# Moving the start addresses of SBUF tiles by four small pads: one operand of the matmuls at 0 modulo 128 bytes, the rest at 64

## The chip, the cores and the metric

The kernel runs on one core of a Trainium2 chip. The time is the device time of one execution in microseconds (us); lower is better. The kernel before took 1770.54 us (median of three runs, 1768.67 to 1771.02).

## The reference

Three stages follow one another; everything is float32.

```python
# 1: attention over keys and values that are means of 8 neighbours (B, H, S, D = 8, 8, 576, 64)
k_p = k.reshape(B, H, Sp, 8, D).mean(axis=3);  v_p = v.reshape(B, H, Sp, 8, D).mean(axis=3)
attn = softmax(q @ k_p.T / sqrt(D));  x = attn @ v_p          # x: 4608 tokens x 512
# 2: x (4608 x 512) -> 2048 -> 512, rational activation
h = x @ w_in
g = (a0 + a1*h + a2*h**2 + a3*h**3) / (1 + |b0|*|h| + |b1|*h**2 + 1e-6)
x = g @ w_out
# 3: 512 -> 1536 -> 512, gated
out = (silu(x @ w_gate) * (x @ w_val)) @ w_out2
```

## The kernel before

Tokens lie along the free axis in nine tiles of 512 (`TT`). A matmul has a **moving** operand, which is streamed column by column (tokens), and a **stationary** one, 128 x 128 weights, which a separate weight load brings in. In the profile's rows of a matmul the names after the arrow are the moving tile and then the stationary one: `bank<-X,W` streams X against W.

Every large product is done three times in a one-pass float32 type (`float32r`): a value is held as a high and a low part in one tile `[128, 2, 512]`, and high x high, high x low and low x high are added up in a PSUM bank. Each of these matmuls reads one contiguous row of 512 columns (2,048 bytes) in each partition of the moving tile, or 256 columns (1,024 bytes) where a stage works on half a token tile. The small matmuls of the attention use plain float32.

There are three phases:

- **Phase 1**, the attention and the second stage of the reference. For each of nine token tiles and 16 slices of the hidden axis (144 steps), 12 matmuls of `proj_ops` stream X against a W tile (`bank<-X,W`, line 473), a chain of ACT, POOL and DVE operations (`moe1_ops`, lines 525 to 547) makes the activation in a tile G, and two steps later 12 matmuls of `acc_ops` stream G against a W tile (`bank<-G,W`, line 473). The attention units (`unit_ops`, `unit_out_ops`; lines 402, 439, 455) for the next token tile, and the conversion of weights (`bits_ops`, `seven_ops`), are put between them.
- **Phase 2** (`pair_ops`, line 684): gate and value projections on pairs of token tiles, in a seven-product scheme. The moving tiles are split tokens; they lie in a ring of slots, X4 to X7 and then fourteen of the W tiles. The stationary tiles lie in the other W tiles, in X0 to X3, in G and in one tile We. So all pairings occur: W against X, W against W, X against X, X against W and a few with G and We.
- **Phase 3** (`out_ops`, line 785): the last projection, with the same slots.

The order of all instructions is set beforehand by a planner (`Plan`): each operation has a due time and a list of engines with costs, and the planner writes one fixed order for each engine. It knows nothing of addresses. All DMAs are issued from SP's queue in that order.

Tiles get their addresses from the order in which they are allocated. `low` (from the bottom) holds `ident`, three small tiles, `X0` to `X7` and the W tiles of the first weight matrix; `low_al` holds the attention's tiles and later W tiles; `const` holds `SA`, `SB`, `SC`, `RAW`, `ST`, four kinds of small tiles, `G0`, `G1` and the W tiles of the second matrix; `al` the last W tiles. Nearly every tile is a multiple of 128 bytes long in a partition, so what a few small tiles leave over is handed on from tile to tile:

```python
    qc = low.tile([128, 1], F32, name="qc")
    X = [low.tile([128, 2, TT], F32R, name=f"X{i}") for i in range(8)]
...
    SM = [const.tile([128, 8, 2], F32, name=f"SM{i}")[:, :, 0:1] for i in range(2)]
    G = [const.tile([128, 2, TT], F32R, name=f"G{i}") for i in range(NG)]
```

The statement that issues nearly all of TensorE's time in phase 1, with w the weights and x the moving tile:

```python
        for j, (i0, i1) in enumerate(((0, 0), (0, 1), (1, 0))):
            nc.tensor.matmul(out=out, lhsT=w[:, i0, wc], rhs=x[:, i1, :],
                             start=first and j == 0, stop=last and j == 2)
```

The diff touches only the allocations at the top of `tile_pooled_attention_moe_moe2`; that function is long, and of it only the pieces above and in the diff matter here.

Of the kernel before, what the change touches and what calls it, by code (L numbers as in the profile page):

```python
# [8 lines left out]
F32 = mybir.dt.float32  # L9
# [61 lines left out]
class Plan:  # L71
# [22 lines left out]
    def op(self, due, alts, r=(), w=()):  # L94
        i = len(self.ops)
        deps = set()
        for k in r:
            if k in self.writer:
                deps.add(self.writer[k])
        for k in w:  # L100
            if k in self.writer:
                deps.add(self.writer[k])
            deps.update(self.readers.get(k, ()))
        deps.discard(i)
        self.ops.append((due, alts, deps))
        for k in w:
            self.writer[k] = i
            self.readers[k] = []
        for k in r:
            self.readers.setdefault(k, []).append(i)  # L110
# [59 lines left out]
def dve(n, fn, port=False, fast=1, ptrs=0):  # L170
    return ("DVE", n / (0.96 * fast) + 66 + 60 * ptrs, 0, port, fn)


def pool(n, fn):
    return ("POOL", 2.1 * n + 145, 0, True, fn)
# [6 lines left out]
def pe(ns, fn):  # L182
    return ("PE", ns, 0, False, fn)
# [3 lines left out]
def tile_pooled_attention_moe_moe2(  # L187
# [18 lines left out]
    low = ctx.enter_context(tc.tile_pool(name="low", bufs=1))  # L206
    low_al = ctx.enter_context(tc.tile_pool(name="low_al", bufs=1))
    const = ctx.enter_context(tc.tile_pool(name="const", bufs=1))
# [8 lines left out]
    ab = low.tile([128, 6], F32, name="ab")  # L217
    babs = low.tile([128, 2], F32, name="babs")
    qc = low.tile([128, 1], F32, name="qc")
    X = [low.tile([128, 2, TT], F32R, name=f"X{i}") for i in range(8)]  # L220
    SCR = tuple(range(32 - NSCR, 32))
    first_use = {f: n for n, (t, f, _, _) in reversed(list(enumerate(SEQ)))}
    need1 = sorted([(first_use[f], "in", f) for f in range(NF1)] + [(first_use[f] + 2, "out", f) for f in range(NF1)])
# [2 lines left out]
    def W(i):  # L226
        if W_[i] is None:
            p = (low_al if i in SCR else low) if need1[i][1] == "in" else (al_p if i in SCR else const)
            W_[i] = p.tile([128, 2, 512], F32R, tag=f"W{i}", name=f"W{i}")
        return W_[i]  # L230
# [5 lines left out]

    scr_tile, scr_keys = {}, {i: [] for i in SCR}

    def scratch(i, key):
        if i not in scr_tile:  # L240
            p = low_al if need1[i][1] == "in" else al_p
            scr_tile[i] = p.tile([128, 1024], F32, tag=f"W{i}", name=f"scr{i}")
        scr_keys[i].append(key)
        return scr_tile[i]
# [7 lines left out]
    MX = [const.tile([128, 8, 1], F32, name=f"MX{i}") for i in range(2)]  # L252

    SM = [const.tile([128, 8, 2], F32, name=f"SM{i}")[:, :, 0:1] for i in range(2)]
    G = [const.tile([128, 2, TT], F32R, name=f"G{i}") for i in range(NG)]
    for i in range(32 - NSCR):
        W(i)
    kpbd = low_al.tile([128, 8, 2, SP], F32, tag="kpbd", name="kpbd")
# [5 lines left out]
    QBS, SSS, ATS = [(QB, "q0")], [(SS, "s0")], [(AT, "at0")]  # L264
    i = SCR[-1]
    QBS.append((scratch(i, "q1")[:, 0:TT], "q1"))
# [15 lines left out]
    class Ring:  # L282
# [17 lines left out]
    first_raw = Ring([  # L300
        (scratch(i, f"fraw{i}").bitcast(I32).rearrange("p (a t) -> p a t", t=2), f"fraw{i}") for i in SCR[4:-3]
    ])
    first_st = Ring(st_all[0:4] + [
        (scratch(i, f"fst{i}{j}")[:, 512 * j:512 * j + 512], f"fst{i}{j}") for i in SCR[0:4] for j in range(2)
    ])
# [54 lines left out]
    def kv_ops(due, bb, hp):  # L360
# [8 lines left out]
        def folds(x, out):  # L369
            for n in (4, 2):  # L370
                P.tensor_tensor(out=x[:, :, 0:n], in0=x[:, :, 0:n], in1=x[:, :, n:2 * n], op=ALU.add)
            P.tensor_tensor(out=out, in0=x[:, :, 0], in1=x[:, :, 1], op=ALU.add)

        op(due, [dve(S, lambda: V.tensor_reduce(out=kt, in_=kr, axis=AX.X, op=ALU.add)),
                 ("POOL", 2.1 * 7 * SP + 435, 0, True, lambda: folds(kr, kt))],
           [], [kk, f"kt{hp % 2}"])
        for h in range(2):
# [5 lines left out]

        op(due + V_POOL, [dve(1024, lambda: V.tensor_reduce(out=vps[:, c], in_=vr, axis=AX.X, op=ALU.add)),
                          ("POOL", 2.1 * 7 * 128 + 435, 0, True, lambda: folds(vr, vps[:, c]))],
           [], [kv, f"vp{c}"])

    def unit_ops(due, t, hp, pa, u=0):
# [4 lines left out]
        m = hp % 2  # L393
        mx, sm = MX[m], SM[m]
        (qb, kq), (ss, ks), (at_, ka) = QBS[u], SSS[u], ATS[u]
        kps = [f"kp{kv_slot(bb, hp)}{h}" for _, _, bb in segs(t, 0, TT) for h in range(2)]
        op(due - Q_DMA, [dma(1 << 18, lambda: sync.dma_start(out=qb, in_=qT[hp, :, t * TT:(t + 1) * TT]))], w=[kq])
        for i in range(2):
# [13 lines left out]
            def peak(g=g, src=src):  # L412
                V.tensor_reduce(out=mx[:, g, :], in_=src, axis=AX.X, op=ALU.max, negate=True)  # L413

# [31 lines left out]
    def unit_out_ops(due, t, hp, pa, u=0):  # L446
# [12 lines left out]

        x = X[(t % 2) * 4 + hp]  # L460
        xk = f"X{(t % 2) * 4 + hp}"
        op(d, [pe(930, pv)], [ka + "a", ka + "b"] + vks, [k0])
# [8 lines left out]
    def mm3(out, w, wc, x, first, last):  # L471
# [4 lines that stand above are left out]
    def proj_ops(due, bk, e, x0):  # L476
        wkey, get = w_tile[e]
        for kt in range(4):
            op(due, [pe(648, lambda kt=kt: mm3(
                bank[bk], get(), slice(kt * 128, kt * 128 + 128), X[x0 + kt], kt == 0, kt == 3))],  # L480
               [wkey + "h", wkey + "l", f"X{x0 + kt}h", f"X{x0 + kt}l"], [f"bank{bk}"])

    def acc_ops(due, e, g, first, last):
        wkey, get = w_tile[e]
        for dt in range(4):
            op(due, [pe(648, lambda dt=dt: mm3(
                bank[PY[dt]], get(), slice(dt * 128, dt * 128 + 128), G[g], first, last))],
               [wkey + "h", wkey + "l", f"G{g}h", f"G{g}l"], [f"bank{PY[dt]}"])

# [26 lines left out]
    def moe1_ops(n):  # L516
        t, f, _, _ = SEQ[n]
        i, g, bk = n % NSC, n % NG, (4 + n % 2 if n < N_SW else 4 + n % 3)
        A, Bt, C, gt, hb = SA[i], SB[i], SC[i], G[g], bank[bk]
        kA, kB, kC, kh = f"A{i}", f"B{i}", f"C{i}", f"bank{bk}"  # L520
        proj_ops(n, bk, ("in", f), (t % 2) * 4)
        if n >= 2:
# [14 lines left out]
            out=gt[:, 0, :], in0=hb, scalar=ab[:, 0:1], in1=Bt, op0=ALU.add, op1=ALU.mult), ptrs=1)],  # L537
           [kh, kB], [f"G{g}h"])
        op(d, [dve(512, lambda: V.scalar_tensor_tensor(  # L539
            out=C, in0=C, scalar=QC, in1=gt[:, 0, :].bitcast(F32), op0=ALU.add, op1=ALU.mult), True)],  # L540
           [f"G{g}h"], [kC])
        op(d, [dve(512, lambda: V.scalar_tensor_tensor(  # L542
# [3 lines left out]
        def low(eng):  # L546
            return lambda: eng.tensor_tensor(out=gt[:, 1, :], in0=A, in1=Bt, op=ALU.mult)  # L547

        op(d, [pool(512, low(P)), dve(512, low(V), True)], [kA, kB], [f"G{g}l"])

# [281 lines left out]
    def w1_ops(i, due, e):  # L832
        if i in SCR:
            op(due, [("NONE", 0, 0, False, lambda: None)], [], scr_keys[i] + [f"W{i}h", f"W{i}l"])
        early = i < 32 - NSCR
        w_ops(due, e, lambda: W(i), f"W{i}", first_raw if early else mid_raw, first_st if early else mid_st)
# [191 lines left out]
```

## Time and profile before

| | |
|---|---|
| median of three runs | 1770.54 us (1768.67 to 1771.02) |
| the profiled execution | 1771.74 us, span 1770.0 us |
| TensorE (PE) busy | 1711.5 us, 97% of the span, 8,100 matmuls |
| weight loads (PEld) busy | 1388.5 us, beside the matmuls |
| VectorE (DVE), ScalarE (ACT), GpSimd (POOL) busy | 1355.1, 1081.5, 512.8 us |
| mean granted TensorE clock | 0.991 of full speed |
| DMA | 283.17 MB, 48.5% of 16 engines over the span |

The busy time of an engine is the union of its instructions, and matmuls overlap in their pipeline: the row of one matmul lasts some 389 ns, while the next one starts earlier. How fast the matmuls follow each other is read from a row of the timeline that merges a run of them, as (length of the run - length of one) / (count - 1).

### The profile page before, as it was taken

The numbers are of one execution on the slowest core, as the hardware profiler recorded it, in microseconds if no ns is written. First come the engines' busy times: TensorE is split into PE (matmuls) and PEld (weight loads), VectorE is DVE, ScalarE is ACT, GpSimd is POOL, SyncE is SP. The second block draws the span as 40 slices with busy tenths as digits, with TensorE's granted clock in tenths as the row PEclk, the third lists the DMA queues.
The fourth block names the chain that finished last, engine by engine and source line by source line (L and its number), as shares of the span: only waits on it lengthen the run. The fifth ranks groups of instructions, "written<-read, shape, count | busy, mean of one in ns | idle before, by whom it ended". The sixth has DMA issues, their size and how long they took to land.

```text
span 1770.0 us, 24470 instructions
## 1 busy us (share of the span) xinstructions
PE 1711.5 (97%) x8100; PEld 1388.5 (78%) x8100; DVE 1355.1 (77%) x2201; ACT 1081.5 (61%) x2324; POOL 512.8 (29%) x424
## 2 busy tenths in 40 slices
PE   5899899999999999999999999999999999999999
PEld 3567677777777787777788777888889888888888
DVE  7899998989989898988999667346354536778874
ACT  7777777777777786777677554334343424545543
POOL 4556463534545362333435121000000000101100
PEclk9799999999999999999999999999999999999999
DMA  8412343514334251313136889546456887755642
GB/s 278 151 42 72 112 145 108 172 45 144 112 116 139 93 158 36 102 49 107 60 119 213 279 281 322 165 143 202 157 173 221 285 265 250 272 182 193 217 135 84
DMA packets 139711, 283.17 MB, mean 160 GB/s; under 512 B 14656, under 2 KB 44864, under 8 KB 139584
## 3 DMA queue, kind: packets, MB, share of 16 engines
q1 hardware_dynamic: 139584, 281.60, 48.5%
q8 instruction: 64, 1.05, 0.2%
q14 instruction: 63, 0.52, 0.1%
HBM read 197.14 MB, written 84.41 MB: 159 GB/s over the span
## 4 chain that ended last, share of the span: by engine, by line
PE 76%; DVE 11%; DMA 6%; ACT 4%; issue 2%; POOL 0%; SPq 0%; DVEq 0%; ACTq 0%; POOLq 0%
PE bank L473 33%; PE bank L684 23%; PE bank L785 15%; DMA wodr<-RAW 2%; PE bank L402 2%; PE bank L455 2%; DVE SC L539 2%; PE bank L439 1%; DVE G L536 1%; DVE SA L542 1%; DVE SA L531 1%; DMA RAW<-in_k 1%; DVE G L547 1%; DVE bank L532 1%; DMA X<-wdr 1%
## 5 line engine op out<-in xcount | busy, mean ns | idle before, releaser
L473 PE MATMUL bank<-X,W 128*128 128x512 f32 x1728 | 442.8, 401 | 7.5 <-DVE SA L542 7.5
L473 PE MATMUL bank<-G,W 128*128 128x512 f32 x1728 | 429.6, 394 | 0.6 <-POOL W L335 0.6
L473 PEld LDWEIGHTS bank<-X,W 128*128 128x128 f32 x1728 | 322.5, 191 | 88.3 <-DVE SA L542 11.5
L473 PEld LDWEIGHTS bank<-G,W 128*128 128x128 f32 x1728 | 319.7, 188 | 72.1 <-issue 5.6
L528 POOL TENSOR_TENSOR SC<-SC,SB 128x512 f32<-128x512 f32 x144 | 198.6, 1379 | 319.0 <-ACT SC L526 317.5
L684 PE MATMUL bank<-W,X 128*128 128x512 f32 (+1 forms) x972 | 213.6, 366 | 3.7 <-ACT SA L693 1.4
L684 PEld LDWEIGHTS bank<-W,X 128*128 128x128 f32 x972 | 169.3, 189 | 35.6 <-ACT ST L693 2.2
L684 PE MATMUL bank<-W,W 128*128 128x512 f32 (+1 forms) x816 | 181.0, 367 | 4.0 <-ACT SB L693 3.0
L785 PE MATMUL bank<-W,W 128*128 128x512 f32 (+1 forms) x840 | 174.8, 365 | 0.0
L684 PEld LDWEIGHTS bank<-W,W 128*128 128x128 f32 x816 | 142.1, 189 | 30.7 <-ACT SB L693 4.0
L785 PEld LDWEIGHTS bank<-W,W 128*128 128x128 f32 x840 | 145.2, 189 | 25.3
L534 ACT ACTIVATE SB<-SC,qc 128x512 f32<-128x512 f32 x144 | 104.6, 726 | 66.8 <-POOL SC L528 66.3
L536 DVE SCALAR_TENSOR_TENSOR G<-bank,ab,SB 128x512 fp32r<-128x512 f32 x144 | 107.4, 746 | 38.8 <-PE bank L473 22.1
L525 ACT ACTIVATE SB<-bank 128x512 f32<-128x512 f32 x144 | 86.0, 597 | 70.5 <-DVE G L547 46.0
L539 DVE SCALAR_TENSOR_TENSOR SC<-SC,G 128x512 f32<-128x512 f32 x144 | 120.6, 837 | 3.8
L526 ACT ACTIVATE SC<-SB,babs 128x512 f32<-128x512 f32 x144 | 117.8, 818 | 0.1
L529 ACT ACTIVATE SA<-bank,ab 128x512 f32<-128x512 f32 x144 | 112.3, 780 | 0.1
L331 POOL TENSOR_TENSOR ST<-ST,ST 128x512 int32<-128x512 int32 x53 | 75.2, 1419 | 115.5 <-DVE ST L328 94.2
L532 DVE SCALAR_TENSOR_TENSOR bank<-SA,ab,bank 128x512 f32<-128x512 f32 x144 | 107.6, 748 | 1.2
L542 DVE SCALAR_TENSOR_TENSOR SA<-bank,ab,SC 128x512 f32<-128x512 f32 x144 | 106.9, 743 | 0.7
L531 DVE TENSOR_TENSOR SA<-SA,bank 128x512 f32<-128x512 f32 x144 | 97.7, 679 | 7.7 <-ACT SA L529 7.4
L417 ACT ACTIVATE QS<-bank,MX 128x72 f32<-128x72 f32 x272 | 83.7, 325 | 21.6 <-DVE MX L413 21.2
(227 smaller groups left out, 2611.5 us busy)
## 6 DMA issues: line engine op xcount, KB each, us to landing
X<-wdr SPq DMA_DIRECT2D x105, 512.0 KB
wdr<-ST SPq DMA_DIRECT2D x84, 256.0 KB
RAW<-sdr SPq DMA_DIRECT2D x56, 256.0 KB
X<-sdr SPq DMA_DIRECT2D x48, 256.0 KB
wodr<-RAW SPq DMA_DIRECT2D x42, 256.0 KB
RAW<-in_w_out SPq DMA_DIRECT2D x19, 512.0 KB
RAW<-in_k SPq DMA_DIRECT2D x32, 288.0 KB
RAW<-in_v SPq DMA_DIRECT2D x32, 288.0 KB
```

The lines of the kernel that those rows point to most:

```text
L473: nc.tensor.matmul(out=out, lhsT=w[:, i0, wc], rhs=x[:, i1, :], start=first and j == 0, stop=last and j == 2)
L526: op(d, [act(512, False, lambda: A_.activation(out=C, in_=Bt, func=AF.Identity, scale=babs[:, 1:2], bias=babs[:, 0:1]), 2)], [kB, "ab"], [kC])
L528: op(d, [pool(512, lambda: P.tensor_tensor(out=C, in0=C, in1=Bt, op=ALU.mult))], [kB], [kC])
L529: op(d, [act(512, True, lambda: A_.activation(out=A, in_=hb, func=AF.Identity, scale=ab[:, 3:4], bias=ab[:, 2:3]), 2)], [kh, "ab"], [kA])
L531: op(d, [dve(512, lambda: V.tensor_tensor(out=A, in0=A, in1=hb, op=ALU.mult))], [kh], [kA])
L532: op(d, [dve(512, lambda: V.scalar_tensor_tensor(out=hb, in0=A, scalar=ab[:, 1:2], in1=hb, op0=ALU.add, op1=ALU.mult), ptrs=1)], [kA], [kh])
L534: op(d, [act(512, False, lambda: A_.activation(out=Bt, in_=C, func=AF.Ln, bias=qc), 1)], [kC], [kB])
L536: op(d, [dve(512, lambda: V.scalar_tensor_tensor(out=gt[:, 0, :], in0=hb, scalar=ab[:, 0:1], in1=Bt, op0=ALU.add, op1=ALU.mult), ptrs=1)], ...
L539: op(d, [dve(512, lambda: V.scalar_tensor_tensor(out=C, in0=C, scalar=QC, in1=gt[:, 0, :].bitcast(F32), op0=ALU.add, op1=ALU.mult), True)] ...
L542: op(d, [dve(512, lambda: V.scalar_tensor_tensor(out=A, in0=hb, scalar=ab[:, 0:1], in1=C, op0=ALU.add, op1=ALU.subtract), ptrs=1)], [kC, k ...
L684: nc.tensor.matmul(out=bk, lhsT=gw()[:, i0, m:m + 128], rhs=gx()[:, i1, 0:n], start=first and kk == 0 and q == 0, stop=kk == 1 and q == 2, ...
L785: nc.tensor.matmul(out=bk, lhsT=gw()[:, g % 2, c:c + 128], rhs=gx()[:, i1, 0:n], start=first and g == 0 and q == 0, stop=g == NFP - 1 and ...
```

## The change

Four pads are allocated and never used: 32 bytes ahead of X, 64 bytes behind X, 64 bytes ahead of G and 64 bytes behind G.

```diff
@@ -217,7 +217,10 @@
     qc = low.tile([128, 1], F32, name="qc")
+
+    low.tile([128, 8], F32, name="pad0")
     X = [low.tile([128, 2, TT], F32R, name=f"X{i}") for i in range(8)]
+    low.tile([128, 16], F32, name="pad1")
     SCR = tuple(range(32 - NSCR, 32))
@@ -252,7 +255,9 @@
     SM = [const.tile([128, 8, 2], F32, name=f"SM{i}")[:, :, 0:1] for i in range(2)]
+    const.tile([128, 16], F32, name="pad2")
     G = [const.tile([128, 2, TT], F32R, name=f"G{i}") for i in range(NG)]
+    const.tile([128, 16], F32, name="pad3")
     for i in range(32 - NSCR):
```

The start addresses in a partition, modulo 128 bytes, in the two built programs:

| tile | before | after |
|---|---|---|
| X0 to X7 | 96 (X0 at 1760) | 0 (X0 at 1792) |
| G0, G1 | 96 | 0 |
| all W tiles, We | 96 | 64 |
| kpbd, vps, QS, AT (attention), scratch | 96 | 64 |
| SA, SB, SC, RAW, ST | 96 | 64 |
| KT0, KT1 | 96, 0 | 64, 96 |
| MX0, MX1; SM0, SM1 | 32, 64; 96, 32 | 0, 32; 64, 0 |
| ident | 0 | 0 |

No instruction is added, removed or moved: the rows of every engine's order, DMAs on SP's queue included, are the same in both programs but for buffer and line numbers. So no excerpt of an order stands here.

## Rows read from the trace of the kernel before

**Rows 1.** The page's part 1: busy time, share of the span, instructions of each engine.

```profile
PE 1711.5 (97%) x8100; PEld 1388.5 (78%) x8100; DVE 1355.1 (77%) x2201; ACT 1081.5 (61%) x2324; POOL 512.8 (29%) x424
```

**Rows 2.** Busy time by stretch: phase 1, phase 2, phase 3.

```profile
core 0: us, PE busy (x) PEld busy (x) DVE busy (x) ACT busy (x) POOL busy (x), PEclk, DMA share, GB/s
33.00:987.00 954.00, 920.94 (x4274) 725.47 (x4273) 864.85 (x1369) 717.37 (x1601) 446.49 (x368) 0.98 0.36 114
987.00:1508.00 521.00, 513.09 (x2484) 431.06 (x2482) 271.52 (x464) 210.88 (x397) 35.88 (x30) 1.00 0.68 227
1508.00:1770.00 262.00, 258.64 (x1260) 219.19 (x1258) 195.87 (x325) 129.38 (x231) 18.50 (x12) 1.00 0.55 179
```

**Rows 3.** The chain that ended last, pieces: start us, us, what.

```profile
860.73 76.52 PE bank L473 x336
...
1507.93 258.72 PE bank L785 x1260
```

**Rows 4.** PE's timeline, runs of 19 (512 columns) and 49 (256 columns).

```profile
1711.77 4.47 PE L785 MATMUL bank<-W,W 128*128 128x512 f32 x19
...
1749.20 6.04 PE L785 MATMUL bank<-W,W 128*128 128x256 f32 x49
```

**Rows 5.** Groups of PE's matmuls by form, lines 473, 684 and 785: busy us, mean ns.

```profile
L473 PE MATMUL bank<-X,W 128*128 128x512 f32 x1728 | 442.8, 401 | 7.5 <-DVE SA L542 7.5
L473 PE MATMUL bank<-G,W 128*128 128x512 f32 x1728 | 429.6, 394 | 0.6 <-POOL W L335 0.6
L684 PE MATMUL bank<-W,X 128*128 128x512 f32 x756 | 183.5, 390 | 2.6 <-ACT SA L693 1.4 <-ACT ST L693 0.6 <-ACT SC L693 0.6
...
L785 PE MATMUL bank<-W,W 128*128 128x512 f32 x648 | 150.8, 389 | 0.0
L684 PE MATMUL bank<-X,X 128*128 128x512 f32 x252 | 67.5, 389 | 0.1
L684 PE MATMUL bank<-X,W 128*128 128x512 f32 x228 | 61.3, 390 | 0.0
L785 PE MATMUL bank<-X,W 128*128 128x512 f32 x216 | 51.9, 389 | 0.0
L402 PE MATMUL bank<-kpbd,QS 128*128 128x144 f32 x240 | 44.8, 305 | 7.6 <-ACT kpbd L379 5.3 <-ACT QS L417 1.8 <-DVE X L466 0.3
L439 PE MATMUL bank<-ident,QS 128*72 128x128 f32 x272 | 42.1, 284 | 23.2 <-POOL QS L431 16.1 <-DVE QS L431 4.6 <-ACT SB L525 1.9
...
L785 PE MATMUL bank<-W,W 128*128 128x256 f32 x192 | 24.0, 283 | 0.0
```

**Rows 6.** PE's timeline, with idle time before; then 54.9 to 57.7 us: timeline, group, stretch.

```profile
47.62 1.92 PE L439 MATMUL bank<-ident,QS 128*72 128x128 f32 x8 [8.07 <-POOL QS L431]
...
54.27 4.04 PE L473 MATMUL bank<-X,W 128*128 128x512 f32 x9
...
L473 PE MATMUL bank<-X,W 128*128 128x512 f32 x9 | 4.0, 628 | 0.0
...
54.90:57.70 2.80, 2.80 (x9) 2.13 (x8) 2.80 (x6) 1.90 (x10) 0.62 (x2) 0.50 0.10 41
```

**Rows 7.** PE's timeline, plain float32: transposes (line 439), scores (line 402).

```profile
503.64 0.60 PE L439 MATMUL bank<-ident,QS 128*72 128x128 f32 x4
...
519.47 0.65 PE L402 MATMUL bank<-kpbd,QS 128*128 128x144 f32 x4
```

**Rows 8.** Groups by line: a DVE operation of phase 1, idle before it, releasers.

```profile
L536 DVE SCALAR_TENSOR_TENSOR G<-bank,ab,SB 128x512 fp32r<-128x512 f32 x144 | 107.4, 746 | 38.8 <-PE bank L473 22.1 <-ACT SB L535 5.7 <-ACT SB L525 4.1
```

**Rows 9.** PE's timeline in phase 2: pairings side by side.

```profile
1450.56 0.84 PE L684 MATMUL bank<-X,X 128*128 128x512 f32 x3
1451.24 0.84 PE L684 MATMUL bank<-W,X 128*128 128x512 f32 x3
```

**Rows 10.** PE's timeline, groups of 12 in phase 1.

```profile
511.13 3.06 PE L473 MATMUL bank<-X,W 128*128 128x512 f32 x12
...
516.75 2.88 PE L473 MATMUL bank<-X,W 128*128 128x512 f32 x12
```

## The prediction

> **What bounds the kernel now.** I read the engines' shares first: PE is busy 97% of the span, the next engine, DVE, 77% [rows 1]. By stretch, PE is the bound in all three phases, but in phase 1 DVE stands close behind it: of 954.0 us PE is busy 920.94 and DVE 864.85; in phase 3 PE is busy throughout and DVE has room [rows 2]. The chain of waits agrees: phase 3 is one piece of 258.72 us of matmuls, and in phase 1 there are pure stretches too, 336 matmuls in 76.52 us [rows 3]. So what the change does to a matmul counts, and the question is how fast matmuls follow each other.
>
> That is read from merged runs. 512 columns: (4.47 - 0.389) / 18 = 0.2267 us. 256 columns: (6.04 - 0.283) / 48 = 0.1199 us [rows 4, 5]. The difference is 106.8 ns for 256 columns, 0.417 ns a column, which is 2.4 GHz. What is left over is 226.7 - 213.3 = 13.3 ns for the long form and 119.9 - 106.7 = 13.3 ns for the short one: **a fixed 13.3 ns per matmul, whatever its length**. There are 6,480 long and 756 short ones in the three phases (lines 473, 684, 785; the largest groups are in [rows 5]), so it costs 7,236 x 13.3 = 96 us in all.
>
> Two rows tell what kind of cost it is. From 54.3 us the granted clock is 0.50, the 1.2 GHz level (PE had stood idle for 8.07 us shortly before), and the same matmul follows after (4.04 - 0.628) / 8 = 426.5 ns [rows 6]: 512 columns at 1.2 GHz are 426.7 ns, so there the extra is gone. And the plain float32 forms take (0.60 - 0.284) / 3 = 105 ns for 128 columns and (0.65 - 0.305) / 3 = 115 ns for 144 [rows 5, 7], about 0.8 ns a column or half the column rate, with no 13 ns on top though each loads its weights too. So the extra is not the hand-over from one matmul to the next. It appears only where 4-byte columns are streamed at full rate, and points at the reading of the operands from SBUF.
>
> **My theory.** At 2.4 GHz 13.3 ns are 32 columns, or 128 bytes of float32. A row of 2,048 bytes that starts at 96 modulo 128 touches 17 blocks of 128 bytes, not 16; one of 1,024 bytes touches 9, not 8: 17 x 32 columns are 226.7 ns and 9 x 32 are 120.0 ns, which are both rows. If the moving row is fetched in such blocks and nothing can run ahead at full rate, a start at 0 gives the extra back, and a start at 64 does not. No row shows it, since all moving tiles of these matmuls start at 96 now.
>
> **The change part by part.** It adds no instruction and moves none; the pads cost nothing in time.
>
> *X and G to 0.* The gain of one matmul lies between 0 (the extra has another cause) and 13.3 ns (all of it goes). The nearest rows are the transposes and scores, where at most 2 or 3 ns can hide in the rounding of the rows [rows 7]; I take 13.3 less about 2, so 11 ns.
>
> Phase 1: 1,728 + 1,728 matmuls [rows 5] x 11 = 38.0 us. Not all will land. DVE's idle time there is 954.0 - 864.85 = 89 us and would shrink to 51, 94% busy, in a fixed order. For it speaks that part of DVE's idle time is itself a wait for PE (22.1 us ahead of line 536 [rows 8]). What is late next is G for the second 12 matmuls. Between 0 and 38 I take two thirds, 25 us.
>
> Phases 2 and 3: moving tiles in X slots are 252 + 228 and 216 long matmuls [rows 5], and seven smaller groups (with G or We, or of 256 columns) add 168: 864 x 11 = 9.5 us. Those of phase 3, 288 x 11 = 3.2 us, land whole, as the chain there is PE alone [rows 3]; of the rest, 6.3 us, I take 5, since the start of phase 2 has gaps that no matmul fills (521.0 us against 513.09 busy [rows 2]). Together 8 us. Moving tiles in W slots (756 and 648 are the largest groups) stay at 226.7 ns.
>
> *Stationary tiles from 96 to 64.* A weight load of 512 bytes touches 5 blocks of 128 either way. I cost it at nothing; what covers it is the matmul beside it (PEld is busy 725.47 us of 954.0 [rows 2]). Bounds: the rivals below, from 5,124 x 11 ns less to 26 us more.
>
> *The tiles of DVE, ACT, POOL and the DMAs from 96 to 64.* Every pairing of tiles on those engines but X and G keeps equal offsets. I cost it at nothing within 2 us either way; the cover is PE, and where DVE's 6% are used up it would show in phase 1.
>
> Sum: 1771.74 - 25 - 8 = 1738.7 us for the profiled execution; this stood 1.2 us above the median of the runs, so **1737.5 us**. The likeliest case's own range: 1771.7 - 47.5 = 1724 where all lands, down to 1753 with 10 us in phase 1 and 7 behind it, or **1722 to 1755**.
>
> **The rivals.**
>
> *Nothing changes (1770.5 us).* The extra belongs to the one-pass float32 form at full clock, wherever its rows start. For it: it is the same for every pairing, in every slot and under every load of the other engines (three matmuls take 0.84 us, or one every 226 ns, for X against X and for W against X [rows 9]). Against it: nothing with another start is among them, so the rows can't tell. The change would then do what it says and be worth nothing. The Trainium skill, "SBUF — State Buffer", section "Specifications (TRN2)", speaks for this rival: the line of SBUF is 16 bytes there, 96, 64 and 0 all start a line, and by that the time would stay at 1770.5. The other way speaks "TensorE: Matmul & The Clock Gate" of the Trainium skill, section "Wait — 56ns, not 53.3ns?": warm matmuls of 512 columns follow after 215.7 ns, and cold ones after exactly N / 1.2 GHz. The cold row agrees (426.5), the warm one does not (226.7). By that page the gain is an estimated 11.0 ns.
>
> *Opposite halves decide (1729 us).* The moving and the stationary row disturb each other where both start at the same offset, and the extra goes wherever they now differ by 64: 3,456 in phase 1, and in phases 2 and 3 W against X 756, X against W 228 + 216, G or We against the other kind 168, short forms 300. That is 1,668 x 11 = 18.3 us behind phase 1, of which 16 land: 1770.5 - 25 - 16. For it: the change keeps its two kinds of tile 64 apart. Against it: the extra has no spread, as two streams that collide at chance should give.
>
> *Any multiple of 64 is enough (1707 us).* All 7,236 matmuls gain: 25 us in phase 1 and 3,780 x 11 = 41.6, of which 38 land.
>
> *Slower (1796 us).* With the two streams at different offsets the weight load takes turns from the stream that it didn't take before, in phase 1 above all, where all 288 groups of 12 have this pairing. The price is bounded below by 0 and above by the slow groups that are there already: 3.06 against 2.88 us for 12 matmuls [rows 10], 0.18 us more, x 288 = 52 us. I take half, 26 us. It decides from 0.012 us per group on, which is 3.5 us or 0.2% of the time.
>
> **How the numbers follow.** Chances: the forecast 0.28, opposite halves 0.15, any multiple of 64 0.14, nothing 0.25, slower 0.18. Of the 0.25 for nothing, 0.01 drifts faster and 0.03 slower by over 0.2%, about what a measurement of this kernel can tell from no change. So faster 0.28 + 0.15 + 0.14 + 0.01 = 0.58, same 0.21, slower 0.18 + 0.03 = 0.21. The range, 1700 to 1782 us, takes in the three gains with their bounds but for the lowest end of the 64 rule, no change, and the mild part of the slower case; about 0.2 is left out.
>
> **What would show it.** Right, if in the profile after: the groups of 12 in phase 1 (X against W, G against W) follow every 215 to 216 ns, a group 2.76 instead of 2.88 us; X against X and X against W do so in phases 2 and 3; and W against X and W against W stay at 226.7. If W against X falls and X against X does not, opposite halves decide; if all fall, 64 is enough. Phase 1 should shrink by some 25 us with DVE at 93% of it. I am wrong if the run of 49 short matmuls and all others still follow every 120.0 and 226.7 ns, or if groups in phase 1 take over 2.9 us.

## The result, and the profile after

The changed kernel takes 1792.58 us (median of four runs, 1788.68 to 1796.16) against 1769.61 us for the kernel before, beside it. The ratio is 1.0123, with a 95% interval of [1.0106, 1.0139]: it is **slower by 23 us**, where 33 us less was forecast. The profiled execution took 1796.16 us, with a span of 1794.4.

The page's part 1 after, then busy time by stretch (phases 1, 2, 3, cut where they end in this trace):

```profile
PE 1739.6 (97%) x8100; PEld 1390.6 (77%) x8100; DVE 1358.6 (76%) x2201; ACT 1081.7 (60%) x2324; POOL 515.6 (29%) x424
```

```profile
35.00:999.00 964.00, 933.32 (x4278) 726.01 (x4277) 869.14 (x1369) 717.54 (x1603) 448.55 (x368) 0.99 0.35 113
999.00:1527.50 528.50, 520.86 (x2481) 430.41 (x2480) 270.43 (x464) 210.90 (x397) 36.53 (x30) 1.00 0.67 224
1527.50:1794.00 266.50, 263.57 (x1261) 219.54 (x1259) 196.24 (x325) 129.25 (x232) 18.55 (x12) 1.00 0.53 175
```

Against [rows 1] only PE has become busier, by 28 us; DVE, ACT, POOL and the weight loads differ by 3.5 us or less. Against [rows 2] phase 1 is longer by 10.0 us, phase 2 by 7.5 and phase 3 by 4.5; the start is later by 2 us. The granted clock is the same to 0.01. So all three phases pay, and they pay on PE.

The chain that ended last after, two pieces that answer to [rows 3]:

```profile
869.27 78.43 PE bank L478 x336
...
1527.65 263.44 PE bank L790 x1260
```

The same 336 matmuls took 76.52 us before, the same 1,260 took 258.72. Nothing waits in these stretches: the matmuls themselves follow each other more slowly. PE's timeline after (start us, us, engine, line, operation, count), in phases 1, 2 and 3:

```profile
883.33 2.95 PE L478 MATMUL bank<-G,W 128*128 128x512 f32 x12
886.12 2.96 PE L478 MATMUL bank<-X,W 128*128 128x512 f32 x12
...
1091.36 5.62 PE L689 MATMUL bank<-X,X 128*128 128x512 f32 x24
...
1471.75 0.86 PE L689 MATMUL bank<-X,X 128*128 128x512 f32 x3
...
1739.82 5.96 PE L790 MATMUL bank<-W,W 128*128 128x512 f32 x25
...
1749.82 2.96 PE L790 MATMUL bank<-W,G 128*128 128x512 f32 x12
...
1760.98 9.42 PE L790 MATMUL bank<-W,W 128*128 128x256 f32 x78
```

A group of 12 in phase 1 takes 2.95 to 2.96 us, where the quick groups before took 2.88 [rows 10]: per matmul (2.96 - 0.398) / 11 = 233 ns against (2.88 - 0.39) / 11 = 226 ns. W against W takes (5.96 - 0.394) / 24 = 231.9 ns, W against G 233 ns. Only the short form is a little quicker, (9.42 - 0.282) / 77 = 118.7 ns against 119.9 [rows 4]. (The last one's length in these sums, 0.389 to 0.398 us for long and 0.276 to 0.283 for short, here and below, is the mean of its form in the trace.)

The surprise is that **hardly any pairing is spared**: moving tiles at 0 are as slow as those at 64, and so are W against W, both at 64. Long runs of X against X do keep the quick pace, 24 in 5.62 us or one every (5.62 - 0.393) / 23 = 227.3 ns; in threes between other pairings they are slow as well, 0.86 us where three took 0.84 [rows 9]. That kills the theory of the prediction at once, but says neither whether the moving start, the stationary start or their relation decides, nor why W against W is slow too.

### The profile page after: what moved, and what is told of

Its sections match the earlier page's. It is cut to its first block, busy times and chain, and to the rows that moved or that the text cites. A ratio compares the mean times of both kernels' runs of the same rounds, so it can differ in the third digit from the quotient of the medians.

```text
span 1794.4 us, 24470 instructions
## 1 busy us (share of the span) xinstructions
PE 1739.6 (97%) x8100; PEld 1390.6 (77%) x8100; DVE 1358.6 (76%) x2201; ACT 1081.7 (60%) x2324; POOL 515.6 (29%) x424
## 4 chain that ended last, share of the span: by engine, by line
PE 79%; DVE 11%; DMA 6%; ACT 3%; issue 2%; POOL 0%; SPq 0%; DVEq 0%; ACTq 0%; POOLq 0%
PE bank L478 36%; PE bank L689 23%; PE bank L790 15%; DMA wodr<-RAW 2%; PE bank L460 2%; PE bank L407 2%; PE bank L444 1%; DVE SC L544 1%; DVE G L541 1%; DVE SA L547 1%; DMA RAW<-in_k 1%; DVE SA L536 1%; DMA ydr<-ST 1%; DMA sdr<-ST 1%; DMA X<-wdr 0%
## 5 line engine op out<-in xcount | busy, mean ns | idle before, releaser
L478 PE MATMUL bank<-X,W 128*128 128x512 f32 x1728 | 448.0, 404 | 7.2 <-DVE SA L547 7.2
L478 PE MATMUL bank<-G,W 128*128 128x512 f32 x1728 | 437.1, 398 | 0.6 <-POOL W L340 0.6
L689 PE MATMUL bank<-W,W 128*128 128x512 f32 (+1 forms) x816 | 183.9, 370 | 3.9 <-ACT SB L698 2.2
L790 PE MATMUL bank<-W,W 128*128 128x512 f32 (+1 forms) x840 | 178.0, 368 | 0.0
L531 ACT ACTIVATE SC<-SB,babs 128x512 f32<-128x512 f32 x144 | 117.8, 818 | 0.1
```

What stands on the lines that cost most here:

```text
L531: op(d, [act(512, False, lambda: A_.activation(out=C, in_=Bt, func=AF.Identity, scale=babs[:, 1:2], bias=babs[:, 0:1]), 2)], [kB, "ab"], [kC])
L689: nc.tensor.matmul(out=bk, lhsT=gw()[:, i0, m:m + 128], rhs=gx()[:, i1, 0:n], start=first and kk == 0 and q == 0, stop=kk == 1 and q == 2, ...
L790: nc.tensor.matmul(out=bk, lhsT=gw()[:, g % 2, c:c + 128], rhs=gx()[:, i1, 0:n], start=first and g == 0 and q == 0, stop=g == NFP - 1 and ...
```

## The experiments

Every kernel here is the kernel before with other pads (or a few edited lines), and with the same order of instructions. `px` and `pw` stand for the bytes of the pads ahead of and behind X, `pg` and `pq` for those ahead of and behind G; the change is 32, 64, 64, 64.

```diff
+    low.tile([128, px // 4], F32, name="pad0")
     X = [low.tile([128, 2, TT], F32R, name=f"X{i}") for i in range(8)]
+    low.tile([128, pw // 4], F32, name="pad1")
...
+    const.tile([128, pg // 4], F32, name="pad2")
     G = [const.tile([128, 2, TT], F32R, name=f"G{i}") for i in range(NG)]
+    const.tile([128, pq // 4], F32, name="pad3")
```

### Which start counts: the moving one, the stationary one, or both

**X and G at 96, the rest at 64** (0, 96, 32, 96).

> X and G stay at 96 modulo 128, all W, attention and scratch tiles go to 64: in phase 1 only the stationary row's start is changed. Moving theory (a long matmul is slow, about 232 instead of 227 ns, when its moving row starts at a multiple of 64): phase 1 (moving X, G) as before at 228 ns; in phases 2 and 3 the W-moving groups at 232, the X-moving ones at 227; about 1781 us. Stationary theory (the same of the stationary row): phase 1 at 232 to 233, W against X at 227, W against W and X against W at 232; about 1793 us. Relation theory (slow when the two starts differ modulo 128): phase 1 and all mixed pairings slow, W against W and X against X at 227; about 1792 us.

1797.13 us, ratio 1.0148 [1.0128, 1.0167]. PE's timeline in phases 1 and 3, and a piece of its chain:

```profile
876.45 2.97 PE L476 MATMUL bank<-G,W 128*128 128x512 f32 x12
879.26 2.97 PE L476 MATMUL bank<-X,W 128*128 128x512 f32 x12
...
1714.77 16.27 PE L788 MATMUL bank<-W,W 128*128 128x512 f32 x69
```

```profile
1528.73 264.34 PE bank L788 x1260
```

**X and G at 0, the rest at 96** (32, 96, 32, 96).

> X and G go to 0 modulo 128, everything else stays at 96. Moving theory: phase 1 at 232 to 233 ns, X-moving groups slow, W-moving ones at 227; about 1789 us. Stationary theory: phase 1 as before at 228, W against X and X against X at 232, W against W at 227; about 1775 us. Relation theory: phase 1 and mixed pairings slow, W against W and X against X at 227; about 1792 us.

1795.07 us, ratio 1.0138 [1.0118, 1.0158]. Timeline and chain:

```profile
877.48 2.97 PE L477 MATMUL bank<-G,W 128*128 128x512 f32 x12
880.28 2.97 PE L477 MATMUL bank<-X,W 128*128 128x512 f32 x12
```

```profile
1524.39 264.34 PE bank L789 x1260
```

These two have no start in common that the other theories could use: modulo 128, once only the stationary tile left 96, once only the moving one. Yet they behave alike, 2.97 us a group and 264.34 us for phase 3 in both. What they share is the difference: moving minus stationary is 32 modulo 128 in both. The moving theory and the stationary theory each missed one of the two by 15 us or more; the relation theory had phase 1 right, but W against W, both at 64, is slow here as well: (16.27 - 0.39) / 68 = 233.5 ns.

**Everything at 0** (32, 0, 0, 0).

> Every large tile at 0 modulo 128, so all pairings have equal starts. Moving theory and stationary theory: all long matmuls at 231 to 233 ns, about 1793 us as with the change. Relation theory: all at 227, about 1770 us. The theory of the prediction (blocks of 128 bytes) would have had 215 ns, and 1707 us.

1769.52 us, ratio 0.9997 [0.9982, 1.0013]: the kernel before again, with X and G exactly where the change puts them. Timeline and chain:

```profile
873.34 2.88 PE L474 MATMUL bank<-G,W 128*128 128x512 f32 x12
876.06 2.88 PE L474 MATMUL bank<-X,W 128*128 128x512 f32 x12
```

```profile
1509.29 258.72 PE bank L786 x1260
```

**Everything at 32** (64, 0, 0, 0).

> Every large tile at 32 modulo 128. If an odd multiple of 32 is what makes the fast state, by the moving or the stationary start: all long matmuls at 227, about 1770 us. Relation theory: the same 1770 us. If the distance to the next multiple of 128 counts (96 is the only good start): slow, 1785 us or more.

1772.56 us, ratio 1.0012 [0.9997, 1.0026]. The chain:

```profile
861.28 76.52 PE bank L474 x336
...
1507.82 258.72 PE bank L786 x1260
```

Both pieces are those of [rows 3] to the hundredth. So where the tiles lie is of no account; **that all of them start alike is what counts**. At 0 the long form follows after the same 226.7 ns as at 96, so a start at a multiple of 128 gives nothing back.

### Alike modulo what

W against W in the change was slow with both at 64 modulo 128. Modulo 256 they are not alike: the four pads leave the W tiles of the lower pools at 64 and those of the upper pools at 192 (X is at 0, G at 128). The pads of the two slow runs above split them too, into 64 and 192 and into 96 and 224. Three kernels test this.

**X and G 128 bytes after all W** (0, 128, 128, 128).

> Moving tiles X and G start 128 bytes further than all W tiles (X 224, G 224, W 96 modulo 256). If the two starts need only be equal modulo 128: every long matmul at 227 ns, about 1770 us. If they must be equal modulo 256: phase 1 at 232 to 234 ns, mixed pairings in phases 2 and 3 slow, W against W at 227 away from the mixed ones; about 1790 us.

1787.27 us, ratio 1.0101 [1.0081, 1.0120]. Timeline in phases 1 and 3, and chain:

```profile
877.05 2.96 PE L476 MATMUL bank<-G,W 128*128 128x512 f32 x12
...
1720.49 2.96 PE L788 MATMUL bank<-X,W 128*128 128x512 f32 x12
...
1727.44 7.88 PE L788 MATMUL bank<-W,W 128*128 128x512 f32 x34
```

```profile
1521.73 260.92 PE bank L788 x1260
```

A difference of 128 is slow, and W against W, now alike modulo 256, is back at (7.88 - 0.39) / 33 = 227.0 ns.

**The change, with all W at 64 modulo 256** (32, 64, 192, 64).

> The change with one difference: modulo 256 X and G start at 0 and all W tiles at 64, where the change has X 0, G 128, the W tiles of the lower pools 64 and those of the upper pools 192. Modulo 128 both kernels are the same. If equality modulo 128 counts: no difference to the change, 1792 us, and W against W stays at 232. If modulo 256: phase 1 stays at 232 to 233 (moving and stationary differ by 64 in both), but W against W, 1,284 long matmuls in phases 2 and 3, falls to 227 where it follows its own kind; up to 6.4 us less, about 1786 to 1789 us.

1789.88 us, ratio 1.0116 [1.0087, 1.0145]. Timeline in phase 3, and chain:

```profile
1651.36 1.54 PE L789 MATMUL bank<-W,W 128*128 128x512 f32 x6
...
1655.54 17.86 PE L789 MATMUL bank<-W,W 128*128 128x512 f32 x78
1673.24 2.96 PE L789 MATMUL bank<-X,W 128*128 128x512 f32 x12
```

```profile
1524.01 260.54 PE bank L789 x1260
```

W against W: (17.86 - 0.39) / 77 = 226.9 ns; X against W beside it stays at 2.96 us. Six of W against W between two groups of X against W are not quick yet, (1.54 - 0.39) / 5 = 230 ns: the disturbance outlasts the pairs that cause it, and a like pair is quick only some matmuls later. Phase 3 is 2.9 us shorter than with the change. The whole time does not tell it from the change (the intervals overlap); the rows do.

**The kernel before with one pad of 128 bytes** (0, 0, 128, 0).

> The kernel before with one pad of 128 bytes ahead of G: G and the upper W tiles go to 96 modulo 256, X and the lower W tiles stay at 224. In phase 1 the two operands of every matmul stay equal modulo 256. If equality modulo 128 counts: 1770 us. If modulo 256: phase 1 as before (228 ns), but the moving lower W tiles against stationary upper W tiles, and X against them, some 1,700 long matmuls in phases 2 and 3, go from 227 to about 232; about 1778 us.

1779.96 us, ratio 1.0054 [1.0037, 1.0071]. Timeline in phases 1 and 3, and chain:

```profile
874.75 2.89 PE L474 MATMUL bank<-G,W 128*128 128x512 f32 x12
...
1640.57 18.29 PE L786 MATMUL bank<-W,W 128*128 128x512 f32 x78
```

```profile
855.51 76.76 PE bank L474 x336
...
1507.26 263.71 PE bank L786 x1260
```

Modulo 128 this kernel is the kernel before. Phase 1, whose pairs stay alike modulo 256, keeps its 2.89 us and 76.76 us; phase 3, where moving lower W tiles meet stationary upper ones, takes 263.71 us, about the change's 263.44, with W against W at (18.29 - 0.39) / 77 = 232.5 ns. So the starts have to be **alike modulo 256**. They need not be alike modulo 512: in the kernel before five W tiles (W20, W22, W24, W26, W28) start at 480 modulo 512 and all other tiles of these matmuls at 224, and yet phase 3, which mixes them, is quick throughout (1,008 x 226.7 + 252 x 120.0 ns make 258.8 us, and [rows 3] have 258.72). This also explains the last riddle of the change: its W against W is slow because its pads split the W tiles into two kinds. And it explains X against X there, alike and quick in a run of 24, slow in threes between unlike pairs.

### Is there a better offset than none

**32 for X and 96 for G** (0, 224, 96, 160).

> A look at two more offsets: X starts 32 bytes after the lower W tiles, G 96 bytes after the upper ones (modulo 256). If only equal starts are fast: X against W and G against W in phase 1 both at 231 to 234 ns, about 1790 us. If some other offset is better than equality, one of the two falls below 226 ns.

1788.89 us (two runs), ratio 1.0109 [1.0078, 1.0140]. Timeline:

```profile
876.76 2.96 PE L476 MATMUL bank<-G,W 128*128 128x512 f32 x12
879.56 2.96 PE L476 MATMUL bank<-X,W 128*128 128x512 f32 x12
```

Both pairings are slow, and neither offset is better than none.

**16 after and 16 before**, by G tiles that are 256 bytes longer:

```diff
-    G = [const.tile([128, 2, TT], F32R, name=f"G{i}") for i in range(NG)]
+    G = [const.tile([128, 2 * TT + 64], F32R, name=f"G{i}")[:, o:o + 2 * TT].rearrange("p (h t) -> p h t", h=2) for i, o in enumerate((4, 60))]
```

> Offsets below 32 bytes: G0 starts 16 bytes after, G1 16 bytes before the upper W tiles modulo 256; X against W stays equal. If only equality is fast: the groups of 12 of G against W at 231 to 234 ns per matmul (2.92 to 2.96 us a group) and their neighbours disturbed, some 6 to 8 us more in phase 1. If a neighbourhood of equality is as good: as before, 2.88 us a group. If a small lead of one side is better: under 2.85 us.

1775.03 us, one run. Four groups in a row, in which G takes turns between its two buffers:

```profile
867.23 2.96 PE L473 MATMUL bank<-G,W 128*128 128x512 f32 x12
870.03 2.88 PE L473 MATMUL bank<-X,W 128*128 128x512 f32 x12
872.75 2.94 PE L473 MATMUL bank<-G,W 128*128 128x512 f32 x12
875.53 2.91 PE L473 MATMUL bank<-X,W 128*128 128x512 f32 x12
```

**8 after and 32 before** (the same edit with 2 and 56).

> The same with G0 8 bytes after and G1 32 bytes before the upper W tiles modulo 256. If only equality is fast: both kinds of group at 231 to 234 ns. If what counts is the line of 16 bytes in which a row starts: G0's groups as before (8 bytes share the line of the start at 224), G1's slow.

1771.96 us, one run. The same place:

```profile
869.80 2.96 PE L473 MATMUL bank<-G,W 128*128 128x512 f32 x12
872.60 2.90 PE L473 MATMUL bank<-X,W 128*128 128x512 f32 x12
875.34 2.96 PE L473 MATMUL bank<-G,W 128*128 128x512 f32 x12
```

Both kinds of G group are slow in both kernels: 8 bytes are as bad as 32, 96 or 128. X against W, which stayed alike, is quick again at once or is disturbed for part of a group. No offset tried beat equality for the long form, and no version here beats the kernel before by more than a measurement can tell. Of the whole time one run says little: these two lie 5.3 and 2.3 us above the median before.

**64 for the short form**, by starting its moving rows 64 bytes into their slot (the same in the two functions that write them and the two matmuls that read them):

```diff
+def at0(n):
+    return 16 if n < TT else 0
...
-        hi, lo = lambda: get()[:, 0, 0:n], lambda: get()[:, 1, 0:n]
+        hi, lo = lambda: get()[:, 0, at0(n):at0(n) + n], lambda: get()[:, 1, at0(n):at0(n) + n]
```

> The kernel before with no pad; the moving rows of the 756 short matmuls (256 columns) start 64 bytes into their slot, so that they lie 64 bytes after the stationary start modulo 256, as W against X and W against G did in the run with X and G at 0 and W at 64, where most short ones of those two pairings took 113 to 114 ns. If the offset decides: short matmuls at 113.3 instead of 120.0 ns; the 252 of phase 3 give 252 x 6.7 = 1.7 us, the 504 of phase 2, which also wait for DMAs, between 0 and 3.4; 1764.5 to 1768 us. If what was seen came from the mixture of pairings: 120 ns and 1769.6 us.

1768.57 us, ratio 0.9996 [0.9984, 1.0008]: no difference. Timeline and chain:

```profile
1743.17 9.35 PE L789 MATMUL bank<-W,W 128*128 128x256 f32 x78
```

```profile
1502.13 258.18 PE bank L789 x1260
```

The short form falls to (9.35 - 0.279) / 77 = 117.8 ns, not to 113.3, and phase 3 gains 0.5 us, not 1.7. A miss: the same difference of 64 gives less here than in the runs from which it was taken. Why is open.

### Where the fixed 13.3 ns come from

**Weight loads of 64 columns in phase 3.**

```diff
-                        nc.tensor.matmul(out=bk, lhsT=gw()[:, g % 2, c:c + 128], rhs=gx()[:, i1, 0:n],
+                        nc.tensor.matmul(out=bk[0:64], lhsT=gw()[:, g % 2, c:c + 64], rhs=gx()[:, i1, 0:n],
```

> The kernel before, but in phase 3 each weight load brings in 64 columns, not 128 (half of the output rows of phase 3 aren't computed; the moving rows are whole). If the fixed 13.3 ns come from the weight load reading beside the stream: they halve, long matmuls at 220.0 and short ones at 113.3 ns, phase 3 shorter by 1,260 x 6.7 = 8.4 us. If they belong to the moving row or the hand-over: 226.7 and 120.0 as before.

1773.77 us, one run. Timeline in phase 3, long and short:

```profile
1640.58 18.10 PE L785 MATMUL bank<-W,W 128*64 128x512 f32 x78
...
1752.18 9.00 PE L785 MATMUL bank<-W,W 128*64 128x256 f32 x78
```

The short form follows after (9.00 - 0.276) / 77 = 113.3 ns: its extra is 6.6 ns, half of the 13.3 that it was. The long form goes the other way, (18.10 - 0.392) / 77 = 230.0 ns. Half the expectation held. The moving rows are as before, so the extra does not belong to them alone. But the edit halves two things at once, the columns of the weight load and the output rows that a matmul writes to its bank, and no run separates the two: that the extra hangs on the weight load is argued, and why the long form became slower is open.

## Why the prediction was wrong

**What held.** PE is the bound in all three phases, and the time of the change is the time between matmuls: all of the loss is there, and no other engine moved by more than 3.5 us. The extra 13.3 ns are real for both lengths, with all starts alike. That they are one fixed cost, and that they come from reading the operands and not from the hand-over, was not shown: with 64 weight columns the short form's extra fell to 6.6 ns, and the long form's rose to 230.0 - 213.3 = 16.7 ns.

**The step that failed** is "X and G to 0": a gain of 11 ns for each moving tile at 0, from the theory that a row starting at 96 touches one block of 128 bytes too many. Everything at 0 has the moving rows just where the theory wanted them, and takes 226.7 ns a matmul and 1769.52 us. The theory fitted two rows exactly (17 x 32 columns, 9 x 32 columns), but these were one number, 13.3 ns, read twice, and all rows had the same start. In its place the runs show that the absolute start is of no account and that the long matmuls leave their quick rhythm, 226.7 ns, for one of 231 to 234 where moving and stationary start differ modulo 256.

**The second failure** is the line that costed the move of the stationary tiles at nothing. It named the cover, the matmul beside it, and the bounds, 26 us slower at the upper end; what the sum left out, and only two of the rivals had, is that the two operands have a relation, which the change broke in all of phase 1 and in most pairs of phases 2 and 3. The table of addresses had shown it: before, all large tiles start alike.

**The rival that came true** is the slower one: two streams at different offsets, 26 us, 1796 us. Its condition and its sign were right. Its mechanism, that the weight load takes turns from the stream, fits but was not shown; its chance was 0.18, and the range stopped at 1782. Its price was right in sum by luck. It put everything into phase 1 (half of 288 x 0.18 us); phase 1 lost 10.0 us, and phases 2 and 3 lost 12.0, for which the rival had no term. The row that it used, 3.06 us for a group [rows 10], is not this effect, as all starts are alike there. That group stands right behind plain float32 matmuls, and so does the next slow one, behind the scores of [rows 7] (timeline before):

```profile
510.12 1.08 PE L455 MATMUL bank<-AT,vps 72*64 72x320 f32 x8
...
519.86 3.03 PE L473 MATMUL bank<-G,W 128*128 128x512 f32 x12
```

The groups that the change made slow take 2.96 us.

**Opposite halves** was the same relation with the wrong sign; **any multiple of 64** and **nothing changes** fell with the result.

Of the pages: "SBUF — State Buffer" of the Trainium skill (section "Specifications (TRN2)") gives lines of 16 bytes, and by that nothing would have changed, since all starts are at the start of a line. The runs differ: one start alone does not matter, but 16 bytes of difference between two operands do, 2.94 to 2.96 against 2.88 us a group, and so do 8. "TensorE: Matmul & The Clock Gate" of the Trainium skill (Part 2, "Step-by-step: what each phase is for") says that weights are read through a port of their own and that loading them steals nothing from the running matmul. The runs speak against it: with half the weight columns (and half the output rows) the short form went from 120.0 to 113.3 ns, and where X stayed in its place and the lower W tiles alone moved against it (X at 96, the rest at 64), X against W went from 2.88 to 2.97 us a group. The measurements decide.

What was not shown: why it is 256 bytes, why 8 bytes are too many, and why a like pair needs some matmuls to become quick again. That the weight load and the moving row disturb each other fits all runs; how they do it stays open.

## What to carry to other kernels

In one-pass float32 matmuls of 512 columns at full clock, each with its own weight load, give moving and stationary tiles start addresses that are equal modulo 256 bytes; a pad, or a small tile put ahead of a large one, that breaks this costs 2 to 3% of every such matmul (1.0 to 1.5% of this kernel's time where all of phase 1 was unlike), without a wait or an idle gap to point at. Look for it in the time between matmuls of a merged run, and list the addresses of the built program modulo 256 whenever an allocation changes. A number that fits two rows is one witness, not two, if both rows come from the same layout.

## What was not expected of the hardware

- The quick rhythm depends on the relation of two addresses: 226.7 ns when alike modulo 256; 231 to 234 ns at every other difference tried in phase 1 (8, 16, 32, 96, 128, 160, 192, 224 and 240 bytes).
- An offset that slows the long form can quicken the short one: 118.7 ns after the change and 117.8 with 64 bytes, against 120.0.
- A like pair between unlike ones is slow as well: three of X against X took 0.86 us in the changed kernel, and 24 in a row 5.62 us, 227.3 ns each.
- A shorter weight load, with half the output rows, does not help the long form: 230.0 ns with 64 columns against 226.7 with 128.
